# One ring of 16 tiles for loaded, transposed and store data, V contracted right after the softmax, order remade

## Chip, cores, metric

One Trainium2 chip, one core. The metric is device time in microseconds (us) of one execution. One profiled execution per kernel gives the trace; its span (first to last instruction) is about 2 us shorter than its time (504.2 of 506.13 us before).

## The reference, cut to what matters

One decode step of an attention layer with a KV cache beside a bilinear MLP, with all gradients. Batch 2, 16 KV heads of 4096 x 128, 32 query heads, bf16:

```python
scores = jnp.einsum("bhqd,bhkd->bhqk", q, k) * (Dh ** -0.5)
p = _softmax(scores, axis=-1)
o = jnp.einsum("bhqk,bhkd->bhqd", p, v)
...
return x + _A_ref(xn, A_k_cache, ...) + _B_ref(xn, B_w_gate, B_w_up, B_w_down)
# outputs: the result and the gradients of x, k_cache, v_cache, wq, wo, w_gate, w_up, w_down
```

K and V are 33.6 MB each and are read once; their gradients are as large and are written once. With the weights and their gradients, 92.5 MB are read and 92.5 MB written.

## The kernel before

It works in 16 steps (8 groups of two KV heads, times 2 of batch). A step loads two K and two V tiles of 1 MB, transposes each on VectorE (DVE), scores them on TensorE (PE), and takes softmax and score gradient (`ds`). It contracts V with the probabilities and K with `ds`, and writes 4 gradient tiles: outer products on PE, evicted from PSUM by ScalarE (ACT) or DVE into a store tile, then stored. Loads and these stores are issued by one queue (SP), in program order: in its trace the queue stood 9.9 us at one load that waited for a transpose, and issued nothing from 345.86 to 355.83 us. GpSimd (POOL) issues most weight loads and weight gradients.

The order of all instructions is worked out while the kernel is built: generators ask for engines, tiles and transfers with estimated costs and priorities, and a small scheduler interleaves them. The priorities were found by search. So any change in the code changes the order of everything after it.

```python
kv_t = tiles("kv", NKV, [P, NCH * Dh])   # 9 loaded tiles, 8 KB per partition
X_t = tiles("X", NX, [P, NCH * Dh])      # 3 transposed
st_t = tiles("st", NST, [P, NCH * Dh])   # 4 store tiles
...
# REL: free when the last reader is done; "lrel": free when the transfer has landed
for j, (dst, src, nbytes) in enumerate(parts):
    yield DMA(engine, 0.77 if engine == "POOL" else 0.45, nbytes)
    ...
yield ("lrel", tag, slot)
...
def contract(s):                          # after ds: V and K in one accumulation
    heads = [(S["ppT"], kvS[s][1][l], l) for l in range(G)] + [(S["ddT"], kvS[s][0][l], l) for l in range(G)]
    for part in range(4):
        for c in range(8 * part, 8 * part + 8):
            for j, (rT, slot, l) in enumerate(heads):
                nc.tensor.matmul(ct[32 * j:32 * j + 32, 0:P], ...)
    for t in range(2):
        for l in range(G):
            yield REL("kv", kvS[s][t][l])
```

## Time and profile before

| | before |
|---|---|
| time, median of the 4 runs beside the changed kernel | 508.33 us (505.04 to 511.59) |
| span of the profiled run | 504.2 us |
| DMA, mean | 369 GB/s |
| missing DMA share (below) | 32.6 us |
| busy DVE / PE / ACT | 390.4 / 373.1 / 301.6 us |

The quantity to watch is the missing DMA share. Cut the span into windows of 8 us, read the DMA share of each, and sum (1 - share) x 8 us where the share is under 1. In the prediction the reader finds the lines that show it, and how one gap arises. An eviction of 128x1024 takes 1.215 us on DVE and 1.016 us on ACT in this trace (means of 82 and 226).

### The profile page before, as it was taken

To read this page: it belongs to the slowest core of one execution; us is meant where nothing else is said; L and a number is where in the kernel's file an instruction comes from. 1 tells how busy PE (TensorE), PEld (TensorE's weight loads), DVE (VectorE), ACT (ScalarE), POOL (GpSimd) and SP (SyncE) were. 2 spreads that over 40 slices of the span, in tenths; PEclk is the share of its full clock that TensorE was granted. 3 is DMA by queue.
4 is the path that set the end of the run, shared out by engine and by line. 5 is a ranking of instruction groups with operands and counts; after the bars stand their busy time and mean duration, and the time that the engine had idled before them with its cause. 6 is when DMAs were issued, how large, how long until landed. Compare 5 with 4: busy or idle time off the path is not lost. (4 is left out here: it accounts for less than half of the span.)

```text
span 504.2 us, 19348 instructions
## 1 busy us (share of the span) xinstructions
PE 373.1 (74%) x8506; PEld 245.7 (49%) x8506; DVE 390.4 (77%) x665; ACT 301.6 (60%) x455; POOL 228.8 (45%) x323
## 2 busy tenths in 40 slices
PE   1558887767775877785886598764988769977886
PEld 0436654444543544453654365543756446553443
DVE  7769988866877899594797678856987678897884
ACT  6137576646464677583684467454675646667873
POOL 6164851443275455242566172552612543664510
PEclk9957567755755766666595656657576555677675
DMA  7997999999899899799999989999899997999886
GB/s 274 402 375 288 386 403 421 411 396 418 317 391 396 331 389 340 281 379 402 412 413 395 409 311 408 327 395 409 287 396 415 411 369 266 393 418 404 338 344 254
DMA packets 34235, 186.19 MB, mean 369 GB/s; under 512 B 4156, under 2 KB 6344, under 8 KB 17768
## 3 DMA queue, kind: packets, MB, share of 16 engines
q1 hardware_dynamic: 22224, 141.25, 70.9%
q0 software_dynamic: 11920, 43.72, 22.6%
q8 instruction: 66, 1.08, 0.8%
q14 instruction: 17, 0.14, 0.1%
q10 hardware_dynamic: 8, 0.00, 0.0%
HBM read 92.48 MB, written 92.48 MB: 367 GB/s over the span
## 5 line engine op out<-in xcount | busy, mean ns | idle before, releaser
L378 ACT CAST st<-ps_o 128x1024 bf16<-128x1024 f32 (+1 forms) x276 | 248.8, 949 | 115.6 <-PE ps_o L1086 43.9
L374 DVE STREAM_TRANSPOSE X<-kv 128x1024 f32<-128x1024 f32 x128 | 156.1, 1229 | 4.7 <-DMA kv<-in_A_k_cache_dram 2.5
L380 DVE CAST st<-ps_o 128x1024 bf16<-128x1024 f32 (+1 forms) x100 | 112.9, 1132 | 51.7 <-DMA out_dram<-st 20.9
L1041 POOL TENSOR_TENSOR BD<-vr,mask 128x2048 bf16<-128x2048 bf16 x32 | 115.2, 3601 | 52.8 <-DVE vr L380 25.3
L600 POOL DMA_DIRECT2D out_dram<-st x43 | 33.1, 770 | 74.5 <-ACT st L378 28.8
L1053 PE MATMUL ps_m<-X,W 128*32 128x128 bf16 x2048 | 63.1, 294 | 5.0 <-issue 2.7
L1086 PE MATMUL ps_o<-BD,pp 32*128 32x512 bf16 x256 | 49.6, 517 | 15.4 <-ACT st L378 7.7
L1086 PE MATMUL ps_o<-BD,dd 32*128 32x512 bf16 x256 | 49.6, 522 | 10.6 <-ACT st L378 7.3
L1053 PEld LDWEIGHTS <-W 128*32 128x32 bf16 x2048 | 48.8, 130 | 17.2 <-issue 15.1
L1227 PE MATMUL ps_m<-kv,dd 128*32 128x128 bf16 x1024 | 55.2, 274 | 2.7 <-issue 2.7
L1227 PE MATMUL ps_m<-kv,pp 128*32 128x128 bf16 x1024 | 55.3, 274 | 1.8 <-issue 1.4
L1227 PEld LDWEIGHTS <-pp 128*32 128x32 bf16 x1024 | 42.3, 123 | 19.3 <-issue 18.4
L1018 POOL COPY W<-rep 32x16 bf16<-32x16 bf16 x128 | 24.9, 194 | 54.8 <-DVE rep L821 44.9
L1227 PEld LDWEIGHTS <-dd 128*32 128x32 bf16 x1024 | 42.0, 123 | 2.1 <-issue 2.1
L374 DVE STREAM_TRANSPOSE X<-ww 128x1152 f32<-128x1152 f32 x25 | 34.1, 1365 | 1.8 <-PE ps_m L837 1.3
L600 POOL DMA_DIRECT2D out_dram<-tl x26 | 14.6, 565 | 30.4 <-ACT tl L378 25.0
L1086 PEld LDWEIGHTS <-pp 32*128 32x128 bf16 x256 | 10.8, 97 | 28.9 <-issue 23.6
L571 POOL COPY wt<-wm 64x128 bf16<-64x128 bf16 (+1 forms) x34 | 8.9, 263 | 32.2 <-DVE wm L565 27.9
L1086 PEld LDWEIGHTS <-dd 32*128 32x128 bf16 x256 | 11.0, 99 | 23.2 <-issue 18.1
L374 DVE STREAM_TRANSPOSE X<-gu 128x1024 f32<-128x1024 f32 x18 | 21.2, 1210 | 0.4 <-PE ps_m L1053 0.4
L696 PE MATMUL ps_m<-gu,xs 128*32 128x128 bf16 x360 | 11.0, 285 | 10.8 <-DMA gu<-in_B_w_up_dram 7.0
L634 PE MATMUL ps_o<-dyr,R 32*128 32x288 bf16 x64 | 10.1, 393 | 10.7 <-ACT st L378 10.0
(202 smaller groups left out, 535.7 us busy)
## 6 DMA issues: line engine op xcount, KB each, us to landing
out_dram<-st SPq DMA_DIRECT2D x64, 1024.0 KB, 6.1
kv<-in_A_k_cache_dram SPq DMA_DIRECT2D x32, 1024.0 KB, 10.9
kv<-in_A_v_cache_dram SPq DMA_DIRECT2D x32, 1024.0 KB, 10.0
out_dram<-st POOLq DMA_DIRECT2D x26, 512.0 KB, 12.2
out_dram<-st POOLq DMA_DIRECT2D x17, 576.0 KB, 9.6
ww<-in_B_w_down_dram SPq DMA_DIRECT2D x9, 576.0 KB, 20.5
ww<-in_A_wo_dram POOLq DMA_DIRECT2D x8, 576.0 KB, 13.6
gu<-in_B_w_gate_dram POOLq DMA_DIRECT2D x9, 512.0 KB, 10.0
```

Of the source, the lines that this page charges most:

```text
L374: nc.vector.transpose(out, in_)
L378: nc.scalar.copy(out, in_)
L380: nc.vector.tensor_copy(out=out, in_=in_)
L571: nc.gpsimd.tensor_copy(view(Wt[:], 64 * h, 64, 0, [[dims[-1][1], n], [1, dims[-1][1]]]), view(Wm[:], 64 * h, 64, off, dims))
L600: (nc.gpsimd if engine == "POOL" else nc.sync).dma_start(dst, src)
L634: nc.tensor.matmul(o[:, aa, 0:HD2], lhsT=lhs(a), rhs=dyr[32 * a:32 * a + 32, k * HD2:(k + 1) * HD2], start=True, stop=True)
L696: nc.tensor.matmul(ug[32 * a:32 * a + 32, 1 - w, :], lhsT=xs[:, dc if dc < 4 else 4 + w, :], rhs=gu[:, FS * k + P * a:FS * k + P * (a + 1) ...
L1018: nc.gpsimd.tensor_copy(view(W_t[t][w][:], 32 * a, 32, 6 + 8 * a, [[G * WW, 4], [WW, G], [1, 2]]), view(rep_t[grp[g]["qs"]][:], 32 * a, 32 ...
L1041: nc.gpsimd.tensor_tensor(BD_t[i][:], view(vr_t[v][:], 0, P, 0, [[0, 16], [1, Dh]]), view(mask16[:], 0, P, 0, [[1, 16], [0, Dh]]), ALU.mult)
L1053: nc.tensor.matmul(sc[32 * cq:32 * cq + 32, :], lhsT=view(W[:], 0, P, (be * G + l) * WW + 6 - 4 * c2 - 2 * l, [[1, 32]]), rhs=view(X[:], 0 ...
L1086: nc.tensor.matmul(o[:, k, :], lhsT=pr2[32 * c4:32 * c4 + 32, :], rhs=BD[32 * c4:32 * c4 + 32, 8 * l + 4 * h2:8 * l + 4 * h2 + 4, :], star ...
L1227: nc.tensor.matmul(ct[32 * j:32 * j + 32, 0:P], lhsT=view(rT, 0, P, 4 * c + 2 * l, [[1, 32]]), rhs=kv_t[slot][:, Dh * c:Dh * (c + 1)], sta ...
```

## The change

Intent: the same 16 tiles serve whoever needs one, so that store tiles in flight needn't come out of 4; V's tiles come free earlier; DVE gets lighter; priorities searched anew.

```diff
-NKV, NX, NGU, NWW, NST, NBD = 9, 3, 1, 5, 4, 3
-MLP0, MLPD = 8, 3.49
+NBIG, NGU, NWW, NBD = 16, 1, 5, 3
+CAP = {"kv": 9, "X": 7, "st": 4}
+MLP0, MLPD = 7, 3.04
-BIAS = 0.15
+BIAS = 0.39            # evictions lean more to ACT
... (slacks and all priorities: new numbers)
-    kv_t = tiles("kv", NKV, ...); X_t = tiles("X", NX, ...); st_t = tiles("st", NST, ...)
+    kv_t = X_t = st_t = tiles("big", NBIG, [P, NCH * Dh])
+    od.share("big", CAP)
...
             elif kind == "lrel":
-                self.slots[s.req[1]][s.req[2]] = s.land
+                self.pool(s.req[1])[s.req[2]] = s.land   # tile: free at landing
+                if s.req[1] in self.used:
+                    self.used[s.req[1]] -= 1             # count: down at issue
...
-        nc.vector.tensor_copy(qd[:, 1], dof[:, :, 0:2])
+        nc.scalar.copy(qd[:, 1], dof[:, :, 0:2])
...
+        yield SPAWN(contract(s, 1), pr("conv", s))       # V: at the end of softmax
-        yield SPAWN(contract(s), pr("con", s))
+        yield SPAWN(contract(s, 0), pr("con", s))        # K: after ds
-def contract(s):
+def contract(s, t):                                      # 64 matmuls each, then a fold of two partial sums
```

More of the change, by code (lines that the diff above doesn't have):

```diff
@@ L86, in __init__ @@
         self.slots = {}
+        self.home, self.cap, self.used = {}, {}, {}
         self.lines = Lines()
@@ L94, in ring, with share, pool @@
         self.slots[tag] = {i: 0.0 for i in range(n)}
+    def share(self, tag, caps):
+        for user, cap in caps.items():
+            self.home[user], self.cap[user], self.used[user] = tag, cap, 0
+    def pool(self, tag):
+        return self.slots[self.home.get(tag, tag)]
     def spawn(self, gen, prio, ready=0.0):
@@ L113, in advance @@
             elif kind == "rel":
-                self.slots[s.req[1]][s.req[2]] = s.ready
+                self.pool(s.req[1])[s.req[2]] = s.ready
+                if s.req[1] in self.used:
+                    self.used[s.req[1]] -= 1
             elif kind == "spawn":
@@ L121, in advance @@
             elif kind == "lrel":
-                self.slots[s.req[1]][s.req[2]] = s.land
+                self.pool(s.req[1])[s.req[2]] = s.land
+                if s.req[1] in self.used:
+                    self.used[s.req[1]] -= 1
             else:
@@ L141, in start @@
         if r[0] == "acq":
-            ts = [when(t) for t in self.slots[r[1]].values() if t is not None]
-            if not ts:
+            ts = [when(t) for t in self.pool(r[1]).values() if t is not None]
+            if not ts or (r[1] in self.used and self.used[r[1]] >= self.cap[r[1]]):
                 return None, None
@@ L182, in run @@
             elif r[0] == "acq":
-                slots = self.slots[r[1]]
+                slots = self.pool(r[1])
+                if r[1] in self.used:
+                    self.used[r[1]] += 1
                 i = min((k for k, v in slots.items() if v is not None), key=lambda k: (when(slots[k]), k))
@@ L246, in DMA @@
     return ("dma", engine, cost, 0.08 + nbytes / 16e3 * packet / row, packet)
-NKV, NX, NGU, NWW, NST, NBD = 9, 3, 1, 5, 4, 3
-MLP0, MLPD = 8, 3.49
+NBIG, NGU, NWW, NBD = 16, 1, 5, 3
+CAP = {"kv": 9, "X": 7, "st": 4}
+MLP0, MLPD = 7, 3.04
 KVSTORE = "SP"
-WQ0, WO0 = -2, -2
+WQ0, WO0 = -3, 0
 LATENCY, DRY = {"SP": 0.6, "ACT": 0.6, "POOL": 2.0}, 0.4
-BIAS = 0.15
-SLACK = {"PE": 0.11, "ACT": 0.21, "DVE": 0.31, "POOL": 0.93, "SP": 5.91}
+BIAS = 0.39
+SLACK = {"PE": 0, "ACT": 0.24, "DVE": 0.42, "POOL": 8.48, "SP": 2.18}
 STEP = 28.0
-HEAD = {"turn0": -96.9, "turn1": -63.0, "att": -34.6, "dsc": -63.3, "con": 2.5, "out1": -1.3, "front": 86.3, "back": 152.3, "W0": 79.2, "W1": 113.2, "BD1": 32.1, "load": 16.8}
-TAIL = {"turn1": 6.7, "att": -0.5, "dsc": -47.3, "con": 173.2, "out1": -11.9, "out0": 27.4, "front": 423.6, "W0": 21.5, "BD1": -20.6, "BD0": 13.1, "load": -7.5}
-PR = {"turn0": 615.2, "turn1": 519.1, "att": -36.4, "dsc": -131.1, "con": 373.1, "out1": 249.7, "out0": 254.3, "front": -120.6,
-      "back": 33.0, "W0": 336.5, "W1": 402.2, "BD1": 480.8, "BD0": 19.3, "mlp": -146.2, "wout": -154.9, "store": 349.0,
-      "load": 650.0, "wload": 29.8, "fin": 213.7, "const": 44.3, "mload": 912.6}
+HEAD = {"turn0": 32.8, "turn1": 5.6, "att": 18.2, "dsc": -4.1, "con": 20.2, "out1": 32.0, "out0": -0.1, "front": 136.3, "back": 186.6, "W0": -106.9, "W1": 1.4, "load": -18.7}
+TAIL = {"turn0": -311.6, "att": -941.4, "dsc": 107.7, "conv": -25.4, "out1": 360.1, "out0": 2.8, "front": 14.6, "back": -0.1, "W0": 72.9, "W1": 0.3, "BD0": -350.1, "load": -45.9}
+PR = {"turn0": 159.1, "turn1": 503.5, "att": -177.4, "dsc": -354.1, "conv": 107.5, "con": 255.2, "out1": 239.8, "out0": 221.8,
+      "front": -254.4, "back": -141.0, "W0": -80.5, "W1": 16.3, "BD1": 432.8, "BD0": -175.2, "mlp": 0.4, "wout": -413.4,
+      "store": 556.3, "load": 796.4, "wload": -183.0, "fin": -239.5, "const": -134.5, "mload": 817.1}
 def pr(name, s):
@@ L325, in tiles @@
         return [const.tile(list(shape), dtype, name=f"{tag}{i}") for i in range(n)]
-    kv_t = tiles("kv", NKV, [P, NCH * Dh])
-    X_t = tiles("X", NX, [P, NCH * Dh])
+    kv_t = X_t = st_t = tiles("big", NBIG, [P, NCH * Dh])
+    od.share("big", CAP)
     Xt_t = tiles("Xt", 1, [P, FS])
@@ L331 @@
     ww_t = tiles("ww", NWW, [P, WB])
-    st_t = tiles("st", NST, [P, NCH * Dh])
     tl_t = tiles("tl", 2, [P, FS])
@@ L350 @@
     dd_t = tiles("dd", 2, [P, 2, P])
-    osb_t = tiles("osb", 1, [P, P])
+    osb_t = tiles("osb", 2, [P, P])
     od.ring("ch", 2)
@@ L397 @@
     eps_t = filled("eps_t", [2, 1], FP32, EPS)
-    oscale = filled("oscale", [P, 1], FP32, 1.0)
-    nc.vector.memset(oscale[64:128], SCALE)
     one1 = filled("one1", [1, 1], FP32, 1.0)
@@ L429 @@
     mask16 = const.tile([P, 16], BF16, name="mask16")
+    fold = const.tile([P, GH], BF16, name="fold")
+    foldf = const.tile([P, GH], FP32, name="foldf")
     Exn, Edy, Econst, Ezero = Event(), Event(), Event(), Event()
@@ L456, in consts @@
                               view(ident[:], 0, P, 0, [[8, 4], [32, 4], [1, 8]]))
+        yield DVE(0.2)
+        sums(foldf[:].rearrange("p (l r) -> p l r", l=2), [[32, 2], [1, 2], [64, 2]])
+        nc.vector.tensor_copy(fold[:], foldf[:])
         yield SET(Econst)
@@ L786, in mlp @@
         yield REL("hb", hs)
-    grp = [dict(Lm=Event(), Eq=Event(), Ed=Event(), Lq=Event(), Lo=Event()) for _ in range(NG)]
-    steps = [dict(done=Event(), outs=[Event(), Event()], sm=Event(), spread=Event()) for _ in range(NS)]
+    grp = [dict(Lm=Event(), Eq=Event(), Ed=Event(), Lq=Event(), Lo=Event(), EoT=Event()) for _ in range(NG)]
+    steps = [dict(done=[Event(), Event()], outs=[Event(), Event()], sm=Event(), spread=Event()) for _ in range(NS)]
     def group_front(g):
@@ L844, in group_front @@
         yield REL("m", m)
-        yield DVE(0.15)
-        nc.vector.tensor_copy(qd[:, 1], dof[:, :, 0:2])
+        yield ACT(0.25)
+        nc.scalar.copy(qd[:, 1], dof[:, :, 0:2])
         yield POOL(0.5)
@@ L855, in group_back @@
         n0 = g * GH * Dh
-        yield WAIT(steps[2 * g]["done"], steps[2 * g + 1]["done"])
+        yield WAIT(*steps[2 * g]["done"], *steps[2 * g + 1]["done"])
         wq, wo, oT = ww_t[st["wq"]], ww_t[st["wo"]], oT_t[st["oT"]]
@@ L1158, in softmax @@
         yield SET(S["sm"])
+        S["pp"] = yield ACQ("pp")
         m = yield ACQ("m")
@@ L1161, in softmax @@
         spread(c["pr"], m_t[m])
-        S["pp"] = yield ACQ("pp")
         e = yield EV(256)
@@ L1195, in dscore @@
         yield REL("m", k)
+        S["dd"] = yield ACQ("dd")
         m = yield ACQ("m")
@@ L1198, in dscore @@
         spread(c["ds"], m_t[m])
-        S["dd"] = yield ACQ("dd")
         e = yield EV(256)
@@ L1211, in dscores @@
             yield from dscore(s)
-    def contract(s):
+    def contract(s, t):
         S = steps[s]
         g, b = divmod(s, Bq)
-        if b == 0:
+        if t == 1 and b == 0:
             grp[g]["oT"] = yield ACQ("oT")
+            yield SET(grp[g]["EoT"])
+        yield WAIT(Ezero, grp[g]["EoT"])
         oT = oT_t[grp[g]["oT"]]
-        yield WAIT(S["spread"], Ezero)
+        i = yield ACQ("osb")
         m = yield ACQ("m")
         ct = m_t[m]
-        heads = [(S["ppT"], kvS[s][1][l], l) for l in range(G)] + [(S["ddT"], kvS[s][0][l], l) for l in range(G)]
-        for part in range(4):
+        rT = S["ppT" if t else "ddT"]
+        for part in range(2):
             yield PE(0.95)
-            for c in range(8 * part, 8 * part + 8):
-                for j, (rT, slot, l) in enumerate(heads):
+            for k in range(8 * part, 8 * part + 8):
+                for j in range(4):
+                    c, l = k + NCH // 2 * (j // 2), j % 2
                     nc.tensor.matmul(ct[32 * j:32 * j + 32, 0:P], lhsT=view(rT, 0, P, 4 * c + 2 * l, [[1, 32]]),
-                                     rhs=kv_t[slot][:, Dh * c:Dh * (c + 1)], start=(c == 0), stop=(c == NCH - 1))
-        for t in range(2):
-            for l in range(G):
-                yield REL("kv", kvS[s][t][l])
-        i = yield ACQ("osb")
+                                     rhs=kv_t[kvS[s][t][l]][:, Dh * c:Dh * (c + 1)],
+                                     start=(k == 0), stop=(k == NCH // 2 - 1))
+        for l in range(G):
+            yield REL("kv", kvS[s][t][l])
         e = yield EV(128)
-        if e == "ACT":
-            nc.scalar.activation(osb_t[i][:], ct[:, 0:P], AF.Copy, scale=oscale[:])
+        if t == 1:
+            cp(e, osb_t[i][:], ct[:, 0:P])
+        elif e == "ACT":
+            nc.scalar.activation(osb_t[i][:], ct[:, 0:P], AF.Copy, scale=SCALE)
         else:
-            nc.vector.tensor_scalar(osb_t[i][:], ct[:, 0:P], oscale[:], None, op0=ALU.mult)
+            nc.vector.tensor_scalar(osb_t[i][:], ct[:, 0:P], SCALE, None, op0=ALU.mult)
         yield REL("m", m)
@@ L1240, in contract @@
         yield PE(0.3)
-        nc.tensor.matmul(m_t[m][:, 0:8], lhsT=osb_t[i][:], rhs=view(ident[:], 0, P, 0, [[32, 4], [1, 2]]),
-                         start=True, stop=True)
+        nc.tensor.matmul(m_t[m][:, 0:GH], lhsT=osb_t[i][:], rhs=fold[:], start=True, stop=True)
         yield REL("osb", i)
         yield DVE(0.19)
-        nc.vector.tensor_copy(view(oT[:], 0, P, b, [[GH * 32, 2], [32, GH]]),
-                              m_t[m][:, 0:8].rearrange("p (t h) -> p t h", t=2))
+        nc.vector.tensor_copy(view(oT[:], 0, P, (1 - t) * GH * 32 + b, [[32, GH]]), m_t[m][:, 0:GH])
         yield REL("m", m)
-        yield SET(S["done"])
-    for j in range(NST):
-        od.slots["st"][j] = None if j < 4 else 0.0
+        yield SET(S["done"][t])
+    od.used["st"] = 4
+    for j in range(4):
+        od.slots["big"][j] = None
     for g in range(NG):
@@ L1287, in final_out @@
         yield PRIO(PR["fin"])
-        yield WAIT(steps[NS - 1]["done"])
+        yield WAIT(*steps[NS - 1]["done"])
         t, e = yield from rows_in(A_x)
@@ L1311, in final_dx @@
         yield PRIO(PR["fin"])
-        yield WAIT(steps[NS - 1]["done"])
+        yield WAIT(*steps[NS - 1]["done"])
         t, e = yield from rows_in(grad_out)
```

## The prediction

> **What bounds the kernel now.** I read the page's head and its 40 slices first, then the busy time of 63 windows of 8 us, then who waited for whom (for the SP queue, ACT and DVE), and last the order in time around the dips. The chain of waits explains 1% of the span here (it follows only the last 7 us), so it decides nothing.
>
> ```profile
> span 504.2 us, 19348 instructions
> PE 373.1 (74%) x8506; PEld 245.7 (49%) x8506; DVE 390.4 (77%) x665; ACT 301.6 (60%) x455; POOL 228.8 (45%) x323
> ...
> DMA  7997999999899899799999989999899997999886
> GB/s 274 402 375 288 386 403 421 411 396 418 317 391 396 331 389 340 281 379 402 412 413 395 409 311 408 327 395 409 287 396 415 411 369 266 393 418 404 338 344 254
> DMA packets 34235, 186.19 MB, mean 369 GB/s; under 512 B 4156, under 2 KB 6344, under 8 KB 17768
> ```
>
> No compute engine is full over the span; the DMA row is at 9 nearly everywhere. The reader is to see the slices where it isn't: the rate falls there from about 400 to under 340 GB/s. With 8 us windows: in 45 of 63 the DMA share is 0.98 or more, at a mean of 398 GB/s. The missing share of the other windows, times 8 us, sums to 32.6 us: 3.4 in the first window, 8.8 after 464 us, 20.3 between. The large ones between are at 40 (3.4), 128 (1.9), 160 (1.7), 200 to 216 (3.1), 288 to 304 (1.8), 320 (1.2), 352 (1.8) and 408 to 424 (4.6). If everything ran at 398 GB/s, 186.19 MB would take 468 us (an estimate); that is the ground that buffers and order can win, and head and tail can't give all of theirs.
>
> What makes a dip? One is seen whole at 344 to 360 us; the columns are busy time of PE, PEld, DVE, ACT, POOL, then granted clock, DMA share, GB/s:
>
> ```profile
> 344.00:352.00 8.00, 2.62 (x76) 1.94 (x74) 3.85 (x10) 2.69 (x5) 1.68 (x4) 0.72 1.02 411
> 352.00:360.00 8.00, 7.33 (x230) 6.15 (x232) 8.00 (x13) 4.20 (x7) 6.62 (x5) 0.50 0.77 261
> ```
>
> ```profile
> 347.28 0.39 DVE L565 TENSOR_TENSOR wm<-ps_m,mask 128x256 bf16<-128x256 f32 x1
> 351.20 0.76 DVE L380 CAST st<-ps_o 128x576 bf16<-128x576 f32 x1 [3.54 <-DMA out_dram<-st]
> ...
> 355.36 0.40 DVE L374 STREAM_TRANSPOSE Xt<-gu 128x256 f32<-128x256 f32 x1
> ```
>
> ```profile
> SPq L979 <- DVE Xt L374: 9.9, 1, 9.9
> ```
>
> DVE (and ACT beside it, 4.07 us) stands still because a store tile has not landed: all four are full. Meanwhile DMA works off its backlog. Then DVE is 8.00 of 8 busy with what it could have done before, the SP queue, which issues in order, waits 9.9 us for one of its transposes, and the DMA falls to 0.77. So an engine stops because DMA is behind, and DMA stops afterwards because the engine is. Over the span these store tile waits are
>
> ```profile
> ACT st L378 <- DMA out_dram<-st: 42.7, 21, 4.5
> DVE st L380 <- DMA out_dram<-st: 20.9, 8, 5.0
> ```
>
> 63.6 us of two engines together, and the SP queue's own waits are mostly for the evictions:
>
> ```profile
> SPq L600 <- DVE st L380: 156.8, 44, 12.3
> SPq L600 <- ACT st L378: 91.8, 29, 14.8
> ```
>
> Most of those 248.6 us are free, as transfers issued earlier still run; only the 20.3 us above cost.
>
> [...] its dips at 160, 288, 352 and 408 us follow waits for a full store ring. [...] The trace has 1.215 and 1.016 us, so moving an eviction from DVE to ACT costs nothing in work.
>
> **The change part by part.**
>
> *One ring.* Before: 9 loaded, 3 transposed, 4 store tiles; after: 16 tiles of the same size with limits 9, 7 and 4. The memory is equal, so no queue can be deeper in all three. But two things open. In the code a user's count goes down when the store is issued, while the tile comes back when it has landed; so the limit of 4 is on tiles being filled, and those in flight don't count. Counting the acquisitions in the built order, only 66 of 156 store tiles take a tile that a store had before, 61 take one that held transposed data and 29 one that held loaded data. Store tiles from the scores' tiles come free by PE, not by a landing. I expect most of the 63.6 us to go: under 20 us left. Transposed tiles reach 4 instead of 3.
>
> *V contracted at once.* The 128 matmuls of a step stay 128, in two halves of 64; a V tile is free after the softmax instead of after the whole score gradient. Cost: 16 more transposing matmuls with their weight loads (0.184 + 0.100 us: 4.5 us of PE), 16 more evictions of 128 columns (0.28 us on DVE: 4.5 us), 16 more small copies (0.176: 2.8 us). Gain: the SP queue now issues 11 loads before its first store instead of 9, so some 2.1 MB more (5 us at 398 GB/s) lie ahead of the dip at 40 us.
>
> *Work moved from DVE to ACT.* Of the 128x1024 evictions DVE had 82 and has 59 in the new order: -23 x 1.215 = -27.9 us; of 128x576, 18 to 15: -2.3; the copy of the output gradient's heads goes to ACT: -8 x 0.687 = -5.5. With the 7.3 added, DVE falls by about 28 to some 362 us, and ACT rises by 23 x 1.016 + 3 x 0.647 + 8 x 0.3 = 28 to some 330 us. Neither then passes 75% of a 490 us span.
>
> *Order.* The store runs of the SP queue between loads were 3, 3, 1, 3, 4, 2, 6, ... and 13 after the last load; they become 2, 1, 2, 1, 2, 2, 1, 4, ... with 10 at the end. A store that isn't ready holds back fewer loads. Loads lead stores by 9.1 instead of 8.9 on the mean, so the lead itself hardly grows. The last MLP slice moves from load 49 to load 62 of 64: its 1.8 MB of output come into the tail. Tail bytes: 13 heads of 1.05 MB and 1.2 MB before, 10 heads, 1.2 and 1.8 MB after: 14.8 to 13.5 MB.
>
> *Sum.* Dips behind full store tiles (160, 288 to 304, 352, 408 to 424) cost 1.7 + 1.8 + 1.8 + 4.6 = 9.9 us; I take 70% off: 7. Of the other 10 between, more even order, the two early loads and the lighter DVE take half: 5. The tail of 8.8 loses 2. Total 14; new waits (below) give back about 1. So 13 us off 507.9 gives 495; I lean 1 us further, since the old order was tuned to the old rings: 494.
>
> **Rivals.** First, *the compute engines stay the bound of the dips*. PE is 8.00 of 8 busy in 416 to 424 at a clock of 0.50, and DVE 8.00 in 352 to 360: if the dips come from bursts of work and not from blocked tiles, deeper buffers shift them only, and the extra PE work counts. Against it: before both of these bursts the same engines idled. Then 501 to 507. Second, *new couplings*: a transpose or a load may now wait for a store's landing (49 transposed tiles and 36 loads take a tile that a store held), which before could not be; SP would then block on landings with everything behind it. For it: both issue in order. Against it: in the built order such a tile was released some 75 or more events earlier. If it bites, 505 to 515. Third, *backlog only moves*: with the DMA share at 1.0, engines that no longer wait for a landing wait for loads instead, and the time falls by just the dips, 4 or 5 us: 503. Fourth, *the tail gets worse*, since MLP output, issued by POOL behind its 3.6 us multiplications, ends late: +4. On the other side, if nearly all dips go and only head and tail stay, 468 + 3.4 + 5 = 476 of span, some 480 of time.
>
> **Range and chances.** 494 us, 481 to 505. The 2% line is 497.8. The three main parts point the same way, and the rivals one and three end within 2%: faster 0.64, same 0.32, slower 0.04.
>
> **What would show it.** Right: waits of ACT and DVE for store landings under 20 us in sum; interior missing DMA share down from 20 to about 8 us; no dip at 40 us; DVE near 362 and ACT near 330 us busy; the full windows still at 398 GB/s. Wrong: the landing waits gone and the dips still there (rival one or three); waits of DVE's transposes or of the SP queue's loads for landings of stores (rival two); a tail with a missing share over 9 us (rival four). What I can't judge is the granted clock, 0.652 on the mean here: if denser work lowers it, PE alone could eat the gain.

## More of the kernel before

Span less missing share is 471.6 us before, and 469 to 484 us in the other traces of this study for which I work it out. That remainder varies by some 15 us and the spans by some 66, so the missing share is most of what kernels differ by.

## The result

| | before | changed |
|---|---|---|
| time, median (range), 4 runs each | 508.33 (505.04 to 511.59) | 493.87 (492.27 to 495.25) us |
| ratio, 95% interval | | 0.9715 (0.9644 to 0.9785) |
| span, profiled run | 504.2 | 493.5 us |
| missing DMA share: total | 32.6 | 23.9 us |
| ... first 8 us / last 40 us, in windows counted back from the end / between | 3.4 / 9.0 / 20.2 | 3.3 / 13.0 / 7.6 us |

A ratio is the mean time of one kernel's runs over that of the other's of the same rounds, so not quite the ratio of the medians. The profiled run of before (506.13 us) was faster than its median, that of the changed kernel (495.25 us) the slowest of its four; that is why the spans differ by 10.7 us and the medians by 14.5.

The page of the changed kernel, head and slices:

```profile
span 493.5 us, 19375 instructions
PE 393.3 (80%) x8522; PEld 255.6 (52%) x8522; DVE 362.6 (73%) x662; ACT 323.4 (66%) x490; POOL 228.2 (46%) x323
...
DMA  7999899999999999999999999999999999998864
GB/s 269 403 382 399 307 371 382 419 415 404 360 390 419 373 330 419 410 404 406 348 374 308 408 421 406 388 418 387 346 419 395 419 423 423 400 420 362 320 266 180
```

The 7s and 8s in the middle of the DMA row are all but gone; the row now falls only at the end, and there earlier than before. Of the 10.7 us of span, 8.7 are missing share (12.6 won between, 4.0 given back in the last 40 us). The remaining 2.0 are a slightly higher rate when DMA runs.

Who waits for a store to land, from the waits of all engines and of the SP queue:

```profile
DVE big L388 <- DMA out_dram<-big: 11.0, 7, 3.3
ACT big L392 <- DMA out_dram<-big: 8.0, 2, 4.8
```

```profile
SPq L617 <- ACT big L392: 105.7, 40, 12.4
SPq L617 <- DVE big L394: 75.3, 19, 11.5
SPq L960 <- DMA out_dram<-big: 52.6, 10, 11.7
```

ACT and DVE waited 63.6 us for landings before and wait 19.0 us now. DVE's 11.0 are of a new kind: L388 is the transposes, which take a tile that a store held. And the SP queue's loads (L960) wait 52.6 us for landings, which before could not happen. That was my second rival; it is real and nearly free. It shows in two dips: at 344 us (1.0 us of missing share), after such a wait of 7.7 us that ended at 344.96 us, and at 56 us, after one of 10.0 us:

```profile
48.00:56.00 8.00, 5.69 (x120) 3.75 (x109) 7.55 (x15) 6.18 (x11) 0.02 (x1) 0.84 0.97 345
56.00:64.00 8.00, 7.34 (x186) 4.84 (x189) 6.62 (x14) 6.25 (x9) 7.81 (x7) 0.71 0.81 286
```

(Columns as in the prediction: busy PE, PEld, DVE, ACT, POOL, then clock, DMA share, GB/s.) This one costs 1.5 us. Why the other waits are free can be read, I think, from the table of transfers, where the last figure is the median time from issue to landing; first the kernel before, then the changed one:

```profile
out_dram<-st SPq DMA_DIRECT2D x64, 1024.0 KB, 6.1
kv<-in_A_k_cache_dram SPq DMA_DIRECT2D x32, 1024.0 KB, 10.9
kv<-in_A_v_cache_dram SPq DMA_DIRECT2D x32, 1024.0 KB, 10.0
```

```profile
out_dram<-big SPq DMA_DIRECT2D x64, 1024.0 KB, 13.2
big<-in_A_k_cache_dram SPq DMA_DIRECT2D x32, 1024.0 KB, 19.0
big<-in_A_v_cache_dram SPq DMA_DIRECT2D x32, 1024.0 KB, 11.9
```

SP's stores and its loads of K take about twice as long although the rate is no lower (mean 369 GB/s before, 377 now). My reading, which no run tests: they stand longer in a fuller queue, and so a load that is issued late still finds DMA at work. It doesn't hold for all transfers: loads of V grew only from 10.0 to 11.9 us, and POOL's stores of 512 KB not at all (12.2 and 11.8). With the medians as means, SP's head stores in flight were 64 x 6.1 / 504 = 0.8 tiles and are 64 x 13.2 / 494 = 1.7 (an estimate). POOL's stores hold about one more tile in both kernels (26 x 12.2 + 17 x 9.6 us before, 26 x 11.8 + 17 x 9.5 us now, over the span). With 2.7 tiles in flight on the mean, four tiles of their own would leave room for little more than one being filled.

### The profile page after: what moved, and what is told of

It reads as the page before. It is cut to its first block, busy times and chain, and to the rows that moved or that the text cites.

```text
span 493.5 us, 19375 instructions
## 1 busy us (share of the span) xinstructions
PE 393.3 (80%) x8522; PEld 255.6 (52%) x8522; DVE 362.6 (73%) x662; ACT 323.4 (66%) x490; POOL 228.2 (46%) x323
## 4 chain that ended last, share of the span: by engine, by line
PE 40%; DMA 24%; DVE 11%; issue 9%; ACT 8%; POOL 5%; SPq 2%; ACTq 0%; POOLq 0%; DVEq 0%
DMA out_dram<-big 16%; PE ps_o L1103 9%; ACT big L392 7%; PE ps_m L1248 7%; PE ps_m L1070 7%; DMA ww<-in_A_wq_dram 6%; DVE big L388 5%; POOL BD L1058 4%; DVE big L394 3%; DMA ww<-in_A_wo_dram 3%; PE ps_o L651 2%; PE ps_o L637 2%; PE ps_m L854 2%; PE ps_m L731 1%; PE ps_m L595 1%
## 5 line engine op out<-in xcount | busy, mean ns | idle before, releaser
L392 ACT CAST big<-ps_o 128x1024 bf16<-128x1024 f32 (+1 forms) x302 | 271.8, 953 | 63.6 <-PE ps_o L1103 38.4
L388 DVE STREAM_TRANSPOSE big<-big 128x1024 f32<-128x1024 f32 x128 | 155.8, 1228 | 16.8 <-DMA out_dram<-big 8.4
L1058 POOL TENSOR_TENSOR BD<-vr,mask 128x2048 bf16<-128x2048 bf16 x32 | 115.3, 3603 | 65.0 <-DVE vr L394 38.4
L394 DVE CAST big<-ps_o 128x1024 bf16<-128x1024 f32 (+1 forms) x74 | 82.6, 1117 | 17.5 <-PE ps_o L1103 7.4
L1070 PE MATMUL ps_m<-big,W 128*32 128x128 bf16 x2048 | 64.2, 295 | 7.0 <-issue 3.7
L1103 PE MATMUL ps_o<-BD,pp 32*128 32x512 bf16 x256 | 55.5, 536 | 8.2 <-ACT big L392 4.9
L1103 PE MATMUL ps_o<-BD,dd 32*128 32x512 bf16 x256 | 55.2, 535 | 4.6 <-ACT big L392 3.1
L617 POOL DMA_DIRECT2D out_dram<-big x43 | 33.1, 771 | 29.8 <-ACT big L392 9.6
L388 DVE STREAM_TRANSPOSE big<-ww 128x1152 f32<-128x1152 f32 x25 | 34.1, 1363 | 8.6 <-DMA ww<-in_A_wo_dram 4.5
L1248 PE MATMUL ps_m<-big,pp 128*32 128x128 bf16 x1024 | 33.7, 304 | 8.3 <-issue 7.0
L1248 PE MATMUL ps_m<-big,dd 128*32 128x128 bf16 x1024 | 31.7, 291 | 6.9 <-issue 5.9
L1248 PEld LDWEIGHTS <-dd 128*32 128x32 bf16 x1024 | 23.5, 130 | 16.0 <-issue 14.8
L388 DVE STREAM_TRANSPOSE big<-gu 128x1024 f32<-128x1024 f32 x18 | 21.8, 1227 | 7.2 <-issue 6.1
L617 POOL DMA_DIRECT2D out_dram<-tl x26 | 14.5, 561 | 15.6 <-ACT tl L392 15.3
## 6 DMA issues: line engine op xcount, KB each, us to landing
out_dram<-big SPq DMA_DIRECT2D x64, 1024.0 KB, 13.2
big<-in_A_v_cache_dram SPq DMA_DIRECT2D x32, 1024.0 KB, 11.9
out_dram<-big POOLq DMA_DIRECT2D x26, 512.0 KB, 11.8
gu<-in_B_w_gate_dram POOLq DMA_DIRECT2D x9, 512.0 KB, 13.2
```

The source lines that it names most:

```text
L388: nc.vector.transpose(out, in_)
L392: nc.scalar.copy(out, in_)
L394: nc.vector.tensor_copy(out=out, in_=in_)
L617: (nc.gpsimd if engine == "POOL" else nc.sync).dma_start(dst, src)
L1058: nc.gpsimd.tensor_tensor(BD_t[i][:], view(vr_t[v][:], 0, P, 0, [[0, 16], [1, Dh]]), view(mask16[:], 0, P, 0, [[1, 16], [0, Dh]]), ALU.mult)
L1070: nc.tensor.matmul(sc[32 * cq:32 * cq + 32, :], lhsT=view(W[:], 0, P, (be * G + l) * WW + 6 - 4 * c2 - 2 * l, [[1, 32]]), rhs=view(X[:], 0 ...
```

## The experiments

Twelve kernels ran, each with 3 rounds against the kernel before. In seven of them one thing is varied while the emission order of the instructions, or the numbers it is made from, is held, because a new order is itself a large change, as the five controls show. "Order kept" means that the list of each engine was compared entry by entry and only tile names differ. Five of the twelve gave wrong results; each is said. The same instructions with the same shapes run in them, but wrong data can also mean a changed wait, and in three of them it did (below).

### Ring and order, each in the other's company

The tile that a user takes is chosen apart from the order (the code in short):

```diff
+class Held:                     # kv_t[i], X_t[i], st_t[i] look up the tile taken
+    def __getitem__(self, i): return self.od.held[self.tag, i]
+    take: the tile of the pool that has been free longest; give: back to its pool
 # old order, one pool:      pools {kv, X, st}: 16
 # new order, three rings:   pools {kv}: 9, {X}: 3, {st}: 4   (borrows 9 times)
 # new order, own store ring: pools {kv, X}: 12, {st}: 4      (borrows once)
```

> The kernel before, every engine's instructions in exactly its order, but each loaded, transposed or store tile is taken from one pool of 16, the one longest free. Theory (tiles): most of the gain is that evictions no longer wait for a store's landing; the landing waits of ACT and DVE fall from 63.6 us to under 20 and the time from 508 to 497 to 502. Rival (order): the gain is in the order of the instructions, which is not touched here; the landing waits fall but the time stays at 505 to 510.

> The changed kernel, every engine's instructions in exactly its order, but the tiles come from three rings of 9 loaded, 3 transposed and 4 store tiles as before (in the few places where the order needs a tile more than its ring has, it borrows one). Theory (tiles): store tiles wait for landings again, over 40 us of such waits on ACT and DVE, and the time goes back to 502 to 508. Rival (order): 493 to 497, the waits are backlog that costs nothing.

> As the run before, but loaded and transposed tiles share 12 and only the store tiles have their own 4. Theory (tiles): nearly as slow as with three rings, 500 to 507, as the store tiles are what matters of the ring. Rival (order): 493 to 496. Rival (loads): if the sharing of loaded with transposed tiles is what matters, it stays at 494 while three rings are slower.

| order | tiles | time | ratio to before | landing waits ACT + DVE | missing share |
|---|---|---|---|---|---|
| old | 9 + 3 + 4 (before) | 508.33 | 1 | 42.7 + 20.9 | 32.6 |
| old | one pool of 16 | 512.59 | 1.014 | 35.5 + 43.1 | 34.1 |
| new | 9 + 3 + 4 (wrong results) | 562.07 | 1.113 | 93.8 + 17.8 | 75.5 |
| new | 12 + 4 | 543.57 | 1.076 | 86.6 + 13.6 | 60.9 |
| new | 16 (changed kernel) | 493.87 | 0.972 | 8.0 + 11.0 | 23.9 |

Neither theory survives as I put it; all three times lie above the ranges of both. The pool on the old order is no gain but 1.4% of loss (interval 1.0109 to 1.0171), outside what either theory expected. Its waits:

```profile
ACT big L411 <- DMA out_dram<-big: 35.5, 14, 5.7
DVE big L407 <- DMA out_dram<-big: 22.9, 10, 5.5
DVE big L413 <- DMA out_dram<-big: 20.2, 7, 4.8
```

The old order has no tile to spare: the evictions (L411, L413) wait hardly less, and the transposes (L407) now wait for landings too. The new order without the pool is far worse than both kernels: with 4 store tiles of their own it waits 100.2 us for landings and loses 50 us:

```profile
ACT st L429 <- DMA out_dram<-st: 86.6, 23, 9.5
DVE st L431 <- DMA out_dram<-st: 13.6, 4, 6.3
```

So of these two orders neither wins without its partner: the new order needs the pool, and the old one gains nothing from it. And of the ring it is mostly the store tiles that count: giving them back their 4 costs 50 of the 68 us that all three rings cost (some 11 of the 68, an estimate, come from a fault, below).

What makes the tiles to spare? In the built order, 36 of the 271 acquisitions in the changed kernel take a V tile between its own contraction and that of its step's K, that is, in the time by which it now comes free earlier. If V were held until K as before, four acquisitions would find 17 or 18 tiles in use. So that order could not be built from 16 tiles without the early V contraction; this part is counted, not run.

### How many tiles stores may rotate through

New order kept, one pool of 16, but stores keep to 6 or 8 of the tiles; the other users prefer the rest and borrow when it is out.

```diff
+mine = [f for f in free if (f.index < 6) == (tag == "st")]     # or 8
+x = longest_free(mine or free)
```

> The changed kernel in exactly its order, one pool of 16, but store tiles may use only 6 of the 16 tiles (loaded and transposed tiles use the other 10 and, when those are out, one of the 6). With 4 it was 543.6, with all 16 it is 493.9. Theory (stores in flight): the time falls with the number of tiles that stores can rotate through, 505 to 520 here, and the landing waits on ACT and DVE lie between 19 and 100 us. Rival (cause elsewhere, the separate rings of loaded tiles): no clear order between 4, 6 and 8.

> The same with 8 tiles for stores. Theory (stores in flight): 495 to 506, below the run with 6. Rival: no clear order; since loaded and transposed tiles then borrow more often, it could even be slower than with 6.

Measured: 521.83 us (ratio 1.029) with 6, 516.08 (1.018) with 8, both with wrong results, and both above the expected range. The landing waits fell as expected: 100.2 us with 4, 60.2 with 6 (46.3 ACT, 13.9 DVE), 49.3 with 8 (38.4, 10.9), 19.0 with all. But there is a flaw in these two runs. In the run with 8, DVE before 46.48 us:

```profile
46.48 1.25 DVE L425 STREAM_TRANSPOSE big<-big 128x1024 f32<-128x1024 f32 x1 [18.83 <-DMA big<-in_A_v_cache_dram]
```

Two windows of the same run, with DMA share and GB/s last:

```profile
40.00:48.00 8.00, 0.16 (x1) 0.00 (x0) 1.52 (x3) 0.00 (x0) 0.00 (x0) 0.50 0.50 206
48.00:56.00 8.00, 7.46 (x135) 5.03 (x136) 7.96 (x14) 5.11 (x7) 4.31 (x5) 0.50 0.09 35
```

The transpose waits 18.83 us for a load that should come after it. This is a latent fault of the changed kernel: V's contraction gives a V tile back without asking whether it has been transposed, and in the built order at least one tile, of step 0, is transposed after it was given back. In the changed kernel nobody takes that tile in between, so its results are right. With other tile choices a later load takes it: the transpose then reads the wrong V, and first waits for it. The three runs with the same relative error, 0.251 in the gradient of K (three rings, 6, 8), have this gap. Their windows at 40, 48 and 56 us miss 12.4 to 13.2 us of DMA share; the changed kernel misses 1.8 us there. Taking the difference off gives, as an estimate, 510 us with 6, 505 with 8 and 551 with three rings; 4 (543.57, right results, no such gap) and 16 (493.87) stand as measured. So the time falls with the tiles that stores can rotate through, as the theory of stores in flight expects. That order holds with and without the correction; the size of the steps hangs on it.

### DVE's share

Emission order and tiles kept, but every so often an eviction of 128x1024 runs on the other engine, 23 in all, which is the difference between the two kernels.

```diff
 e = yield EV(cols)
+if cols == 1024: e = turned(e)      # every 11th of ACT's to DVE; or 23 of DVE's 82 to ACT
 ev(e, o_t[i])
```

> The changed kernel, its emission order and tiles kept, but 23 of ACT's 128x1024 evictions, evenly spread, run on DVE, so that DVE has 82 of them as before. Theory (DVE was near its limit): DVE busy some 391 us again, time 500 to 507. Rival (the share of DVE never bound): 493 to 497.

> The kernel before, emission order and tiles kept, but 23 of DVE's 82 evictions of 128x1024, evenly spread, run on ACT. Theory (DVE was near its limit): DVE busy some 362 us, time 499 to 504. Rival (the share of DVE never bound, or an eviction out of its place costs as much as it saves): 505 to 511.

New kernel with DVE heavier: 504.99 us, ratio 0.995 (0.9881 to 1.0015), DVE 387.9 us busy, missing share 32.1 us. Old kernel with DVE lighter: 509.35, ratio 1.004 (0.9978 to 1.0109), DVE 365.7 us, missing share 32.6 us. In the new kernel moving the evictions back costs 0.995 / 0.972 = 2.4%, in the range of the theory; in the old one a lighter DVE gives nothing, as the rival said. What an eviction out of its planned place costs by itself, I can't separate in either run, so that the lighter DVE is worth 2.4% is not shown.

The two runs also part the landing waits from the time. The new kernel with DVE heavier waits 19.6 us in sum, hardly longer than the changed one, and yet misses 8.2 us more of DMA share:

```profile
DVE big L388 <- DMA out_dram<-big: 12.5, 9, 2.6
ACT big L392 <- DMA out_dram<-big: 7.1, 2, 4.3
```

The old kernel with DVE lighter waits 49.8 us instead of 63.6 and gains nothing. So few landing waits are not enough for the gain, and fewer of them don't always bring one.

### Controls: other orders

Priorities moved at random (by at most 3 for the new, 8 for the old kernel), and one version in which V's tiles are given back only when transposed:

```diff
+if t == 1: yield WAIT(*xE[s][1])     # the safe version
 for l in range(G): yield REL("kv", kvS[s][t][l])
-PR = {"turn0": 159.1, "turn1": 503.5, ...}
+PR = {... each + uniform(-3, 3)}     # the moved ones
```

> The changed kernel with every priority of its order moved by a random amount of at most 3 (of hundreds): a control for what another order of the same quality does by itself; it differs from about the twelfth store on. Theory (tiles): the gain doesn't hang on the one order found, 492 to 499. Rival (order): the numbers were searched for this very order, and another one loses half of the gain, 499 to 505.

> The changed kernel with one wait more in its order: V's tiles are given back only when they have been transposed too (in the changed kernel as it is, one V tile is given back by its contraction before it has been transposed; its data survive because nobody takes the tile in between; in two runs before somebody did, and results were wrong). The order parts from the changed kernel's after the 16th load or store. Right results expected. Theory (search): an order nobody searched for: 500 to 515. Rival (structure): 493 to 499.

> The same safe version with priorities moved by at most 3 at random. Theory (search): 500 to 515, and the new structure's moved orders are on the mean some 5 to 15 us below the old structure's moved orders if the structure is worth anything by itself. Rival (structure): 493 to 499.

> The kernel before with every priority moved by at most 8 at random, an order that parts from its own at the third store: the control that the old rings lack. Theory (search): the old order was searched for the old rings as the new one was for the new; both lose about as much when moved: 510 to 522. Rival (structure): the old structure has less to lose, 505 to 510, and the new structure's moved order at 514 is bad luck.

> A second such control for the kernel before, parting after some 22 loads and stores. Theory (search): 510 to 522. Rival (structure): 505 to 510.

| structure, order | time | ratio | results |
|---|---|---|---|
| new, moved | 514.42 | 1.018 | wrong (step 5: the V fault above, by the built order) |
| new, safe wait | 543.87 | 1.069 | right |
| new, safe wait, moved | 533.12 | 1.047 | right |
| old, moved | 520.10 | 1.023 | right |
| old, moved (another) | 544.70 | 1.072 | wrong (cause not traced) |

An order that nobody searched for costs 2 to 7% over the kernel before, in either structure. Only the first of the two old ones fell in a range that I expected; the other four came out slower than both theory and rival. Three new ones average 530 us and two old ones 532: with this few, they don't differ. So a claim like "the structure is worth x by itself" can't be drawn from them. Nor does any run search longer for an order of the old structure; that the new priorities are merely the better search stays an open rival for part of the gain. The safe version shows how such a loss looks. For 32.1 us SP's queue stands before one MLP load, from its waits:

```profile
SPq L996 <- DVE Xt L388: 32.1, 1, 32.1
```

The window of the same run:

```profile
440.00:448.00 8.00, 6.42 (x132) 4.56 (x127) 7.09 (x16) 2.81 (x7) 0.14 (x1) 0.71 0.01 2
```

The next transfer in line waits for the MLP's only weight tile to be transposed, and everything behind it in that queue waits with it. POOL's queue doesn't fill in: it stands 32.0 us before a store of its own, which waits for ACT, until 447.86 us. The DMA share is 0.01 for these 8 us. That is a defect of the order that came out; what the added wait costs by itself is not shown.

No experiment beat both kernels.

## Why the prediction was right, and where its steps were not

It said 494 us, 481 to 505; measured were 493.87. By its steps:

- **Interior dips.** Predicted: 20 us to about 8. Measured: 20.2 to 7.6, and the dip at 40 us gone (1.02 of DMA share in 40 to 48 us), though 1.8 us are missing from 48 to 64 us. Right.
- **Landing waits of ACT and DVE.** Predicted under 20 us; measured 19.0. Right. That they cost is shown only for the new order: there, restoring them to 100.2 us costs 50 us. On the old order a pool doesn't remove them, and the run with DVE heavier loses 11 us with as few of them as the changed kernel.
- **How the 14 us were put together.** I gave 7 us to the store tiles and 5 to order, early loads and DVE, as if they could be added up. The runs show no such parts: pool alone +1.4%, order with 12 + 4 tiles +7.6% and with three rings +11%, lighter DVE alone +0.4%. The working is wrong there, and that the sum met the time within 1 us is partly luck: the interior came out as predicted, but the tail was off by 6 us (below), and what made up for it are the higher rate and the difference between profiled runs and medians.
- **Tile counts.** "66 of 156", "61", "29", and 49 and 36 for transposed tiles and loads are a miscount: the listing held one and a half builds. One build has 107 store tiles, 45 from a store, 41 from transposed data, 20 from loaded and one unused; 35 of 98 transposed tiles and 17 of 66 loads take a store's tile. The shares hardly change.
- **DVE and ACT.** Predicted 362 and 330 us; measured 362.6 and 323.4. One term was misread: the copy of 128x8 that moved to ACT has a mean of 0.687 us on DVE but a median of 0.174. One of the eight took 3.10 us from 124.28 us on and ended at 127.38 us; a GpSimd multiplication of 3.60 us, begun at 123.74 us, ended at 127.34 us. Whether one held the other up, no view shows. On ACT all eight take 0.20 to 0.23 us.
- **PE.** Predicted + 4.5 us, measured + 20.2. The added matmuls are there, but 9.4 us are the split contraction itself (55.8 to 65.2 us for the same 2048 matmuls) and 9.6 the outer products, which the change doesn't touch (98.1 to 107.7). The granted clock fell from 0.652 to 0.623 in these two profiles, as I had feared; with 0.623 to 0.651 over the four runs of the changed kernel, all within 492.27 to 495.25 us, it did not eat the gain. The clock alone doesn't tell these times. In the groups of the pages, by `pp` and `dd`, where overlap counts twice, the outer products take 49.6 + 49.6 us before and 55.5 + 55.2 in the changed kernel; at 0.642 the old kernel with DVE lighter takes 53.1 + 50.4, at 0.641 the new one with DVE heavier 56.0 + 55.1. What adds to them isn't settled.
- **Tail.** Predicted 2 us better, with rival four at + 4. Measured 4.0 us worse in the last 40 us: rival four. From 464 us on:

```profile
464.00:472.00 8.00, 6.50 (x198) 4.09 (x190) 5.64 (x12) 4.32 (x6) 1.11 (x2) 0.71 0.63 220
472.00:480.00 8.00, 6.71 (x123) 3.90 (x116) 5.57 (x9) 7.04 (x11) 0.73 (x3) 0.71 0.83 331
480.00:488.00 8.00, 6.64 (x60) 4.02 (x59) 4.11 (x12) 3.12 (x6) 1.84 (x3) 0.50 0.59 217
```

No engine is full; PE is the nearest, with 6.6 of 8. POOL's last multiplication had begun at 453.8 us, so POOL's multiplications are not what holds the tail, as I had put it. SP's stores wait 18.4 us there for evictions (15.8 by DVE, 2.6 by ACT). That the late MLP slice is the cause is argued, not shown.

- **The rate.** Full windows were to stay at 398 GB/s and came to 405.
- **New couplings** cost me 1 us of the sum. They showed as 52.6 us of waits and two dips of 1.5 and 1.0 us: about right in size. My reason, that such tiles were given up long before, can't be the whole of it, as the waits are there; that a fuller queue covers for them is a reading, not shown.

## What to carry to other kernels

Where transfers bound a kernel, count the missing DMA share, not the waits: 52.6 us of new waits cost some 2.5 us, and 63.6 us of old ones could not be removed by the shared tiles alone. Here a shared pool paid only together with an order built for it, which takes tiles that are given back earlier; test buffers and order apart, with the order held, before crediting either. If the order of a kernel was found by search, run a few unsearched orders as controls, and check that no tile is given back before its last reader, since a lucky order hides such a fault.
